# Three held stores behind the last loads in GpSimd's ring, batch 3's first MLP layer in four pieces, the two last stores in halves

## The chip, the cores and the metric

The kernel runs on one core of a Trainium2 chip. The metric is device time in microseconds, the median of several runs. The core has a matmul engine (TensorE, PE), VectorE (DVE), ScalarE (ACT), GpSimd (POOL) and SyncE (SP), and 16 DMA engines that carry what GpSimd's ring (queue q0) and SP's ring (queue q1) hand them.

## The reference

For each of 4 batches, a cross-covariance attention over q, k, v of 6208 x 256, and then a two-layer MLP on the 128 rows with the highest scores:

```python
def _attn_ref(q, k, v, tau):
    qn = q / (np.linalg.norm(q, axis=1, keepdims=True) + 1e-06)
    kn = k / (np.linalg.norm(k, axis=1, keepdims=True) + 1e-06)
    s = kn.transpose(0, 2, 1) @ qn / tau
    ...
    a /= a.sum(-1, keepdims=True) + 1e-09
    return (v @ a).astype(np.float32)

def _moe_ref(x, w_gate, w1, w2, capacity):        # capacity 128
    ...
        top_idx = np.argpartition(-scores[b], capacity)[:capacity]
        xe = x[b, top_idx]
        h = np.maximum(xe @ w1, 0.0)
        ye = h @ w2
        g = 1.0 / (1.0 + np.exp(-scores[b, top_idx]))
        out[b, top_idx] = x[b, top_idx] + g[:, None] * ye
```

## The kernel before

A batch of 6208 rows is cut into six chunks of 1024 rows (1 MB in f32) and one of 64. The order of chunks is `order = [0, 6, 1, 2, 3, 4, 5]`, so `LAST` is chunk 5 and `order[-2]` chunk 4. `L` is batch 3, `E` batch 2. For each batch all q and k chunks are loaded first and summed into the two Gram products in PSUM (`p1_row`); then the softmax; then all v chunks are loaded, transposed (`p2_transpose`), scored (`p2_score`) and multiplied by the attention matrix (`p2_out`), and ScalarE copies the result to a `stage` tile (L482), from which it is stored. Loads are GpSimd's and convert f32 to bf16 on the way, so a load reads 1 MB and writes 512 KB. The last v chunks of batch 3 are loaded in halves.

When a batch's scores are there, `select_stages` finds the 128 rows, gathers them (L603, GpSimd), runs the MLP on them (L641 to L666) and writes the updated rows to the output with a scatter (L697, GpSimd). The scatter of a batch must wait until the stores of this batch have landed. For batch 3, SP waits for the last transfers (`nop`, L691) before the scatter. The first layer of the MLP has eight matmuls into each of two PSUM tiles of 512 columns; for batch 3 ScalarE evicts the first (L651) and VectorE the second (L653).

Stores are SP's. Those of batches 2 and 3 are held back: none is issued until a certain load has landed (`GATE` in `out_store`, in the kernel before the first half of chunk 4 of batch 3's v). Two chunks of batch 1 (`late`) get their MLP update within the matmuls (`change`, `one_hot`, L479) and are stored last of all, so batch 3's scatter doesn't wait for them. From the gate on, SP's ring gets in order: batch 2's chunk 0 in halves, its 64 rows, its chunks 1 to 5, batch 3's chunk 0, 64 rows, chunk 1, chunks 2 and 3 in quarters, chunks 4 and 5, and the two late chunks of batch 1: fourteen times 1 MB and two small pieces. A ring has eight semaphores in turn, so an issue also waits until the transfer eight issues before it in its ring has landed.

The order of instructions on each engine is made by a planner in the program itself (the loop from L843 on): it keeps clocks of the engines (`vt_clock`) and of the rings (`Rings`) and takes what is due next. `r` in that loop is when the planner expects a piece of input. So a changed constant can move instructions.

Of the kernel before, what the change touches and what calls it, by code (L numbers as in the profile page):

```python
# [14 lines left out]
AF = mybir.ActivationFunctionType  # L15
# [3 lines left out]
P = 128  # L19
# [8 lines left out]
def kernel(  # L28
# [12 lines left out]
    nc = tc.nc  # L41
# [8 lines left out]
    NFC = F // P  # L50
    NFULL = N // CHUNK
    REM = N - NFULL * CHUNK
# [34 lines left out]
    def view(t, b, ci):  # L87
        if t is out:
            rows = outs_of[b][b * N:(b + 1) * N]
            if ci < NFULL:  # L90
                return rows[ci * CHUNK:(ci + 1) * CHUNK].rearrange("(p s) c -> p s c", s=RPP)
            return rows[NFULL * CHUNK:N]
        if ci < NFULL:
            return t[b, ci * CHUNK:(ci + 1) * CHUNK, :].rearrange("(p s) c -> p s c", s=RPP)
        return t[b, NFULL * CHUNK:N, :]


    order = [0, NFULL] + list(range(1, NFULL))
    FIRST, LAST = order[0], order[-1]
    L = B - 1  # L100
    E = B - 2
# [7 lines left out]
    UNIT = 2.46  # L109
# [39 lines left out]
    rings = Rings()  # L149
    vt_clock = {"pe": 0.8, "dve": 0.8, "act": 0.8, "pool": 0.8, "sp": 0.8}  # L150

    def now():
        return vt_clock["pe"]
# [6 lines left out]
    late = [(1, order[-2]), (1, LAST)]  # L160
# [42 lines left out]
    def pump():  # L203
        rings.run(now())
        flying[:] = [key for key in flying if rings.done.get(key, 1.0e9) > now()]
        while nxt_unit[0] < len(units):
            u = units[nxt_unit[0]]
            if in_use[bucket(u)] >= limit[bucket(u)] or len(flying) >= AHEAD:
# [13 lines left out]
                      in_=moe_w1.rearrange("(dc p) f -> p dc f", p=P))  # L222
# [59 lines left out]
    stored = {b: [] for b in range(B)}  # L282
# [4 lines left out]
    gate_done = []  # L287
# [158 lines left out]
    def out_psum():  # L446
        turn[0] += 1
        if acc_dead[0]:
            if turn[0] % 4 == 1:
                return ps_s.tile([P, 2, C], F32, name="s_ps")  # L450
            if turn[0] % 4 == 3:
                return ps_g.tile([P, 4, P], F32, name="g_ps").rearrange("p a c -> p (a c)").rearrange(
                    "p (a c) -> p a c", a=2)
        return ps_o.tile([P, 2, C], F32, name="o_ps")
# [26 lines left out]
                                     stop=pj == m - 1 and cc == 1)  # L481
        nc.scalar.copy(st[:parts, s0 + pair * 2:s0 + pair * 2 + m, :], o_ps[:parts, :m, :])  # L482

    def emit_store(b, ci, parts):
        st = stage_of.pop((b, ci))
        ins = []
        keep = dmas if (b, ci) not in late else []
        if ci < NFULL:
            for h in range(parts):
                rows = slice(h * RPP // parts, (h + 1) * RPP // parts)  # L490
                ins.append(nc.sync.dma_start(out=view(out, b, ci)[:, rows, :], in_=st[:, rows, :]))
        else:
            ins.append(nc.sync.dma_start(out=view(out, b, ci), in_=st[:REM, 0, :]))
        if (b, ci) not in late:
            held[b] -= 1
        keep.extend(ins)
        return ins[0]

    def select_stages(b):
# [32 lines left out]
        for i in range(NSTEP):  # L532
# [16 lines left out]
            for h in range(7):  # L549
# [4 lines left out]
                                    in_=mps[:, 0:7 * NTHR].rearrange("p (s j) -> p j s", s=7),  # L554
# [40 lines left out]
        if b == late[0][0]:  # L595
# [7 lines left out]
        ins = nc.gpsimd.indirect_dma_start(out=vg, out_offset=None, in_=v_flat,  # L603
                                     in_offset=bass.IndirectOffsetOnAxis(ap=idx[:, 0:1], axis=0))
# [23 lines left out]
        for cc in range(2):  # L628
            nc.tensor.matmul(mps[:, 0:C], lhsT=vgt[:, cc, :], rhs=a_sb[:, cc, :], start=cc == 0,
                             stop=cc == 1)  # L630
# [7 lines left out]
        nc.vector.tensor_tensor_reduce(out=scj, in0=xe, in1=wg_bcast, scale=1.0, scalar=0.0,  # L638
                                       op0=ALU.mult, op1=ALU.add, accum_out=ssc)
        h_sb = moe.tile([P, NFC, P], BF16, name="h_sb")  # L640
        for hf in range(NFC // 4):  # L641
            h_ps = out_psum().rearrange("p a c -> p (a c)")
            for f4 in range(4):
                fc = hf * 4 + f4
                for dc in range(2):
                    nc.tensor.matmul(h_ps[:, f4 * P:(f4 + 1) * P], lhsT=w1_sb[:, dc, fc * P:(fc + 1) * P],
                                     rhs=xet[:, dc, :], start=f4 == 0 and dc == 0,
                                     stop=f4 == 3 and dc == 1)
            hv = h_sb[:, hf * 4:(hf + 1) * 4, :].rearrange("p f t -> p (f t)")
            if hf == 0 or b < L:  # L650
                nc.scalar.activation(hv, h_ps, AF.Relu)  # L651
            else:
                nc.vector.tensor_scalar_max(hv, h_ps, 0.0)  # L653
        vt_clock["act"] = max(vt_clock["act"], now() + 0.6) + (0.8 if b == L else 1.4)
        gate = moe.tile([P, 1], F32, name="gate")
        nc.scalar.activation(gate, ssc, AF.Exp, scale=-1.0)
# [2 lines left out]
        for fc in range(NFC):  # L659
            nc.tensor.matmul(y_ps[:, 0, :], lhsT=h_sb[:, fc, :], rhs=w2_sb[:, fc, :], start=fc == 0,  # L660
                             stop=fc == NFC - 1)
# [27 lines left out]
        if b == L:  # L689

            nop = nc.sync.nop()  # L691
            for d in dmas[-20:]:
# [4 lines left out]
        ins = nc.gpsimd.indirect_dma_start(out=outs_of[b][0:(b + 1) * N, :],  # L697
                                           out_offset=bass.IndirectOffsetOnAxis(ap=idx[:, 0:1], axis=0),
                                           in_=upd, in_offset=None)
# [93 lines left out]
    def stage_ready():  # L793
        if len(stage_keys) < ST_BUFS:
            return 0.0
        key = stage_keys[-ST_BUFS]
        if key in stage_free:
            return stage_free[key]
        return rings.landing(("st",) + key) + 0.3

    GATE1 = ("v", E, LAST, 0)
    GATE = ("v", L, order[-2], 0)

    def out_store(b, ci):
        vt_clock["sp"] = max(vt_clock["sp"], vt_clock["act"]) + 0.1
        gate = None
        if (b, ci) == hold1[0]:
            gate = GATE1
        elif b >= E and not gate_done:
            gate_done.append(1)  # L810
            gate = GATE
        if gate:
            vt_clock["sp"] = max(vt_clock["sp"], rings.landing(arrival_key[gate]))
        parts = 1 if ci == NFULL else 4 if b == L and ci in order[3:5] else 2 if 0 < len(gate_done) < 3 else 1
        if gate_done:
            gate_done.append(1)
        key = ("st", b, ci)
        for h in range(parts):
            rings.add(1, vt_clock["sp"] + 0.85, UNIT / parts if ci < NFULL else 0.2, key)
        if (b, ci) not in late:  # L820
            stored[b].append(key)
        st = emit_store(b, ci, parts)
        if gate:
            tc.add_manual_dep(
                st.ins, half_inst[gate].ins.name,
                mybir.DependencyInfo(mybir.DependencyClass.Sync, mybir.DependencyReason.DATA),
                reason="stores behind loads")
# [15 lines left out]
    while True:  # L843
# [11 lines left out]
        if nxt_unit[0] == len(units) and not drained and E in gathered:  # L855
            nc.gpsimd.drain(fusable=False)
            drained = True
        while deferred and (GATE1 if deferred[0] in hold1 else GATE) in half_inst:
            out_store(*deferred.pop(0))
        t = now()  # L860
# [3 lines left out]
        if eat_at < len(eat):  # L864
            kind, u, x = eat[eat_at]
            if u in loaded:
                row = x if kind == "p1" else x[1]
                r = rings.landing(arrival_key[u + (int(row >= RPP // 2),)]) + 0.1
                if acc_dead[0]:
                    r += -0.7 if u == ("v", L, LAST) else 0.7  # L870
                if kind == "p1":
                    if u[2] == FIRST and x == 0:
                        r = max(r, acc_free[0])
                else:
                    r = max(r, min(vt_bank)) if vt_live < VT_BUFS or acc_dead[0] else FAR
                able.append((r, 0.5 if acc_dead[0] else 2, kind))
        if score_at < len(scores):
            b, g = scores[score_at]
            if b in aw_ready and (b, g) in vts:
                able.append((max(aw_ready[b], vt_ready[(b, g)]), 1, "S"))  # L880
        if out_at < len(outs):
            b, g, pr = outs[out_at]
            if b in a_ready and (b, g) in vts and score_at > gs.index(g) + b * len(gs) and (
                    (b, g[0]) not in late or hot):
                r = max(a_ready[b], vt_ready[(b, g)], min(o_bank))
                if g[0] < NFULL and g[1] == 0 and pr == 0:
                    r = max(r, stage_ready())
                if eat_at < len(eat) and eat[eat_at][0] == "p1" and b == E and r < t + 1.0:
                    arr = able[-1][0] if able and able[-1][1] == 2 else FAR
                    if max(r, t) < arr < max(r, t) + 0.5:  # L890
                        r = FAR
# [10 lines left out]
        if fit:  # L902
            r, prio, what = min(fit, key=lambda a: (a[1], a[0]))
# [5 lines left out]
        else:  # L909
            r, prio, what = min(able, key=lambda a: (a[0], a[1]))  # L910
# [8 lines left out]
            t = r  # L919
# [10 lines left out]
        elif what == "p1":  # L930
            _, u, s = eat[eat_at]
# [12 lines left out]
        elif what == "T":  # L944
            _, u, g = eat[eat_at]
# [24 lines left out]
        elif what == "S":  # L970
            b, g = scores[score_at]
# [9 lines left out]
        else:  # L981
            b, g, pr = outs[out_at]
# [50 lines left out]
```

## Time and profile before

| | us |
|---|---|
| median of 3 runs | 258.89 |
| the runs | 258.16, 258.89, 259.0 |
| profiled execution, whole | 257.59 |
| its span, first to last instruction | 255.9 |
| PE busy | 214.0 (84%) |
| ACT busy | 106.5 (42%) |
| DVE busy | 92.4 (36%) |
| POOL busy | 56.9 (22%) |
| GpSimd's ring, share of 16 DMA engines' span | 76.4% |
| SP's ring, the same | 26.7% |
| HBM read and written | 78.91 MB and 25.95 MB, 410 GB/s |

The span is one profiled execution; the runs are timed without a profile. Shares of DMA engines can be a little over 1, because the packets of one engine overlap at their ends. The granted clock of TensorE was 0.977 of full speed over the span.

### The profile page before, as it was taken

The page shows a single profiled execution, that of the slowest core. Times are in us where ns is not written, and L with a number is a line of the kernel's source. Part 1 is how long each engine was busy: PE and PEld are TensorE (multiplying, and loading weights), DVE is VectorE, ACT ScalarE, POOL GpSimd, SP SyncE. Part 2 cuts the span into 40 slices and gives each one's busy share as a digit, 9 for nine tenths or more (in the row PEclk, how much of TensorE's full clock was granted, in tenths as well). Part 3 has the DMA queues.
Part 4 walks back from the last instruction along what each step waited for, and adds up shares of the span by engine and source line. Part 5 has one row for each costly group of instructions (what it writes and reads, how often), then busy time and mean ns, then how long its engine had stood idle before and what let it go on. Part 6 is the DMA issues. An engine that isn't in the chain of part 4 may idle for free.

```text
span 255.9 us, 6666 instructions
## 1 busy us (share of the span) xinstructions
PE 214.0 (84%) x2878; PEld 187.4 (73%) x2878; DVE 92.4 (36%) x409; ACT 106.5 (42%) x186; POOL 56.9 (22%) x106
## 2 busy tenths in 40 slices
PE   0099877899999539989999789899999999999960
PEld 0069767798878539878888678788898878888840
DVE  2000001725552002545645006546751064488130
ACT  3800002754554102584234005774313069697740
POOL 7323110522005100722201404112313310000301
PEclk9999999999999958999999999999999999999996
DMA  6999999999999999999999999999999999999996
GB/s 240 258 216 215 214 214 211 215 207 247 272 318 316 315 295 213 224 215 211 264 279 254 214 210 214 213 272 308 219 213 219 214 209 239 415 423 406 376 425 252
DMA packets 17903, 66.88 MB, mean 261 GB/s; under 512 B 2129, under 2 KB 3666, under 8 KB 15058
## 3 DMA queue, kind: packets, MB, share of 16 engines
q0 software_dynamic: 12672, 38.93, 76.4%
q1 hardware_dynamic: 5202, 27.53, 26.7%
q8 instruction: 22, 0.36, 0.5%
q14 instruction: 7, 0.06, 0.1%
HBM read 78.91 MB, written 25.95 MB: 410 GB/s over the span
## 4 chain that ended last, share of the span: by engine, by line
DMA 60%; PE 26%; issue 4%; DVE 4%; POOL 2%; ACT 1%; POOLq 1%; DVEq 0%
DMA k_ch<-in_k_dram 40%; DMA q_ch<-in_q_dram 17%; PE s_ps L303 4%; PE o_ps L474 4%; PE vt_ps L403 4%; DMA out_dram<-stage 3%; PE g_ps L307 2%; PE g_ps L305 2%; PE sc_ps L440 2%; PE g_ps L474 2%; PE s_ps L474 1%; PE o_ps L841 1%; POOL q_ch L187 1%; PE m_ps L550 1%; ACT e L357 1%
## 5 line engine op out<-in xcount | busy, mean ns | idle before, releaser
L303 PE MATMUL s_ps<-q_ch,k_ch 128*128 128x256 bf16 x384 | 90.6, 280 | 27.8 <-DMA k_ch<-in_k_dram 27.8
L305 PE MATMUL g_ps<-q_ch 128*128 128x128 bf16 x384 | 85.8, 224 | 0.0
L307 PE MATMUL g_ps<-k_ch 128*128 128x128 bf16 x384 | 85.8, 223 | 0.0
L482 ACT COPY stage<-o_ps 128x512 f32<-128x512 f32 x77 | 43.9, 589 | 44.0 <-PE o_ps L474 41.7
L303 PEld LDWEIGHTS <-k_ch 128*128 128x128 bf16 x384 | 38.4, 100 | 30.6 <-DMA k_ch<-in_k_dram 29.8
L307 PEld LDWEIGHTS <-k_ch 128*128 128x128 bf16 x384 | 38.6, 100 | 5.4
L305 PEld LDWEIGHTS <-q_ch 128*128 128x128 bf16 x384 | 38.4, 100 | 0.1
L474 PE MATMUL o_ps<-a_sb,vt_sb 128*128 128x256 bf16 (+1 forms) x250 | 35.5, 272 | 1.0 <-ACT stage L482 0.5
L317 DVE CUSTOM_DVE_ANT_0 junk<-g_ps,ident_f 128x128 f32<-128x128 f32 x16 | 4.7, 291 | 67.4 <-PE g_ps L307 67.0
L474 PEld LDWEIGHTS <-vt_sb 128*128 128x128 bf16 (+1 forms) x264 | 23.7, 97 | 6.6 <-issue 3.3
L403 PE MATMUL vt_ps<-ident_b,v_ch 128*128 128x128 bf16 x360 | 25.4, 219 | 2.8 <-ACT vt_sb L417 2.5
L403 PEld LDWEIGHTS <-v_ch 128*128 128x128 bf16 x384 | 23.2, 97 | 5.1 <-issue 3.9
L313 ACT COPY s_sb<-s_ps 128x512 f32<-128x512 f32 x4 | 2.3, 586 | 56.5 <-PE s_ps L303 56.5
L187 POOL DMA_DIRECT2D v_ch<-in_v_dram x26 | 14.2, 547 | 45.2 <-PE vt_ps L403 18.2
L417 ACT COPY vt_sb<-vt_ps 128x1024 bf16<-128x1024 bf16 (+1 forms) x26 | 22.6, 927 | 2.9 <-PE vt_ps L403 2.9
L187 POOL DMA_DIRECT2D q_ch<-in_q_dram x25 | 13.9, 557 | 29.6 <-DMA q_ch<-in_q_dram 10.0
L841 PE MATMUL o_ps<-w_sb,ident_b 128*128 128x256 bf16 x124 | 18.8, 272 | 0.2 <-ACT h_sb L651 0.2
L187 POOL DMA_DIRECT2D k_ch<-in_k_dram x25 | 13.6, 543 | 23.6 <-DMA v_ch<-in_v_dram 9.6
L603 POOL DMA_INDIRECT vg<-in_v_dram,idx x4 | 4.0, 1008 | 63.2 <-DVE idx L599 33.8
L534 DVE SCALAR_TENSOR_TENSOR cmp<-sc,wl,tab 128x392 bf16<-128x392 f32 x28 | 17.5, 626 | 1.0
L841 PEld LDWEIGHTS <-ident_b 128*128 128x128 bf16 x124 | 10.7, 97 | 1.3 <-issue 0.4
L553 DVE TENSOR_REDUCE cnt<-m_ps 128x8 f32<-128x56 f32 x28 | 6.1, 216 | 15.3 <-PE m_ps L550 14.9
(189 smaller groups left out, 270.7 us busy)
## 6 DMA issues: line engine op xcount, KB each, us to landing
out_dram<-stage SPq DMA_DIRECT2D x21, 1024.0 KB, 10.6
q_ch<-in_q_dram POOLq DMA_DIRECT2D x23, 512.0 KB, 17.2
k_ch<-in_k_dram POOLq DMA_DIRECT2D x23, 512.0 KB, 18.8
v_ch<-in_v_dram POOLq DMA_DIRECT2D x22, 512.0 KB, 14.8
stage<-in_moe_w_dram SPq DMA_DIRECT2D x2, 1024.0 KB, 7.0
out_dram<-stage SPq DMA_DIRECT2D x8, 256.0 KB, 8.1
v_ch<-in_v_dram POOLq DMA_DIRECT2D x4, 256.0 KB, 11.2
out_dram<-stage SPq DMA_DIRECT2D x2, 512.0 KB, 5.3
```

What stands on the lines that cost most here:

```text
L187: ins = nc.gpsimd.dma_start(out=t[:, rows, :], in_=view(src, b, ci)[:, rows, :])
L303: nc.tensor.matmul(s_ps[:, cc, :], lhsT=ks[:, sl], rhs=qs, start=begin and cc == 0, stop=end and cc == 1)
L305: nc.tensor.matmul(g_ps[:, cc, :], lhsT=qs[:, sl], rhs=qs[:, sl], start=begin and cc == 0, stop=False)
L307: nc.tensor.matmul(g_ps[:, 2 + cc, :], lhsT=ks[:, sl], rhs=ks[:, sl], start=False, stop=end and cc == 1)
L403: nc.tensor.transpose(vt_ps[:, cc, j, :parts], in_=vt[:parts, s0 + j, cc * P:(cc + 1) * P], identity=ident_b[:parts, :parts])
L417: nc.scalar.copy(vt_sb[:, :, :n, :parts], vt_ps[:, :, :n, :parts])
L440: nc.tensor.matmul(sc_ps[:parts, first + j, :], lhsT=vt_sb[:, cc, j, :parts], rhs=aw_sb[:, cc, :], start=begin and cc == 0 and j == 0, sto ...
L474: nc.tensor.matmul(o_ps[:parts, pj, :], lhsT=vt_sb[:, cc, j, :parts], rhs=a_sb[:, cc, :], start=pj == 0 and cc == 0, stop=pj == m - 1 and ...
L482: nc.scalar.copy(st[:parts, s0 + pair * 2:s0 + pair * 2 + m, :], o_ps[:parts, :m, :])
L534: nc.vector.scalar_tensor_tensor(out=cmp, in0=sc[:, 0:NCOL, None].to_broadcast([P, NCOL, NTHR]), scalar=wl[:, i, NTHR:NTHR + 1], in1=tab[: ...
L553: nc.vector.tensor_reduce(out=cnt9[:, 0:NTHR], in_=mps[:, 0:7 * NTHR].rearrange("p (s j) -> p j s", s=7), axis=AX.X, op=ALU.add)
L841: nc.tensor.matmul(o_ps[:, 0, :], lhsT=ident_b, rhs=w2_sb[:, 0, :], start=True, stop=True)
```

## The change

There are three edits and one constant.

- `emit_store` takes the queue that issues. The first three stores of batch 2 (chunk 0, now whole, the 64 rows, and chunk 1) are issued by GpSimd, so that they stand in its ring behind the last loads, without a gate. SP's first held store is now batch 2's chunk 2, and its gate is the last half of the last load (`("v", L, LAST, 1)`).
- The first MLP layer of batch 3 (`b == L`) is written in four pieces of 256 columns, each in a PSUM tile of its own; ScalarE evicts pieces 0 and 2, VectorE 1 and 3. The other batches keep two of 512.
- The two late stores of batch 1, the last in SP's ring, go in halves.
- In the planner the expected arrival of the last v chunk is 0.4 us after the estimate instead of 0.7 us before it.

```diff
-    def emit_store(b, ci, parts):
+    def emit_store(b, ci, parts, queue):
...
-                ins.append(nc.sync.dma_start(out=view(out, b, ci)[:, rows, :], in_=st[:, rows, :]))
+                ins.append(queue.dma_start(out=view(out, b, ci)[:, rows, :], in_=st[:, rows, :]))
...
-        for hf in range(NFC // 4):
+        piece = 2 if b == L else 4
+        for hf in range(NFC // piece):
             h_ps = out_psum().rearrange("p a c -> p (a c)")
-            for f4 in range(4):
-                fc = hf * 4 + f4
+            for f4 in range(piece):
+                fc = hf * piece + f4
...
-            hv = h_sb[:, hf * 4:(hf + 1) * 4, :].rearrange("p f t -> p (f t)")
-            if hf == 0 or b < L:
-                nc.scalar.activation(hv, h_ps, AF.Relu)
+            hv = h_sb[:, hf * piece:(hf + 1) * piece, :].rearrange("p f t -> p (f t)")
+            if hf % 2 == 0 or b < L:
+                nc.scalar.activation(hv, h_ps[:, 0:piece * P], AF.Relu)
             else:
-                nc.vector.tensor_scalar_max(hv, h_ps, 0.0)
+                nc.vector.tensor_scalar_max(hv, h_ps[:, 0:piece * P], 0.0)
...
-    GATE = ("v", L, order[-2], 0)
+    GATE = ("v", L, LAST, 1)
+
+    BEHIND = 3
+    behind = []
 
     def out_store(b, ci):
+        if b >= E and len(behind) < BEHIND:
+            behind.append((b, ci))
+            key = ("st", b, ci)
+            vt_clock["pool"] = max(vt_clock["pool"], vt_clock["act"]) + 0.6
+            rings.add(0, vt_clock["pool"] + 1.0, UNIT if ci < NFULL else 0.2, key)
+            stored[b].append(key)
+            emit_store(b, ci, 1, nc.gpsimd)
+            return
...
-        parts = 1 if ci == NFULL else 4 if b == L and ci in order[3:5] else 2 if 0 < len(gate_done) < 3 else 1
-        if gate_done:
-            gate_done.append(1)
+        parts = 1 if ci == NFULL else 4 if b == L and ci in order[3:5] else 2 if (b, ci) in late else 1
...
                 if acc_dead[0]:
-                    r += -0.7 if u == ("v", L, LAST) else 0.7
+                    r += 0.4 if u == ("v", L, LAST) else 0.7
```

On GpSimd, at the end of the loads (`v_ch` are the last v chunks, `vg` is batch 3's gather), the difference of the two programs is:

```order
 L187 DMA v_ch<-in_v_dram 128x2048 x3
 L187 DMA v_ch<-in_v_dram 128x1024 x4
+L491 DMA out_dram<-stage 128x2048
+L493 DMA out_dram<-stage_rem 64x256
+L491 DMA out_dram<-stage 128x2048
 L603 DMA vg<-in_v_dram,idx 128x256
```

Three stores now stand between the last load and the gather of batch 3.

On SP, from batch 1's stores to the end (128x2048 is a whole store of 1 MB, 128x1024 a half, 128x512 a quarter):

```order
 L491 DMA out_dram<-stage 128x2048 x6
 L493 DMA out_dram<-stage_rem 64x256
-L491 DMA out_dram<-stage 128x2048 x3
-L491 DMA out_dram<-stage 128x1024 x2
-L493 DMA out_dram<-stage_rem 64x256
-L491 DMA out_dram<-stage 128x2048 x6
+L491 DMA out_dram<-stage 128x2048 x8
 L493 DMA out_dram<-stage_rem 64x256
 L491 DMA out_dram<-stage 128x2048
 L491 DMA out_dram<-stage 128x512 x8
```

Two halves, a 64-row piece and one whole store have left SP's row; behind what is shown, four whole stores have become two whole ones and four halves.

On VectorE, in batch 3's MLP (`scj` is the gate's dot product, `h_sb` the first layer's output):

```order
 L638 ISA scj,ssc<-xe,wg_bcast 128x256
 L638 ISA ssc 128x1
-L653 TENSOR_SCALAR h_sb<-g_ps 128x512
-L662 TENSOR_SCALAR gate<-gate 128x1
-L663 RECIPROCAL gate<-gate 128x1
-L665 SCALAR_TENSOR_TENSOR upd<-o_ps,gate,xe 128x256
-L1028 UNCONDITIONAL_BRANCH
+L654 TENSOR_SCALAR h_sb<-g_ps 128x256
+L654 TENSOR_SCALAR h_sb<-s_ps 128x256
```

One eviction of 512 columns has become two of 256, and what follows them is the same but for its line numbers.

## Rows read from the trace of the kernel before

**Rows 1.** The page, part 2: busy tenths of the DMA engines in 40 slices.

```profile
DMA  6999999999999999999999999999999999999996
```

**Rows 2.** Stretches: window, us, busy us (x instructions) of PE, PEld, DVE, ACT, POOL, clock, DMA share, GB/s.

```profile
205.00:212.00 7.00, 6.53 (x79) 5.51 (x77) 5.10 (x27) 5.24 (x11) 1.06 (x2) 1.00 1.06 210
214.50:215.00 0.50, 0.50 (x10) 0.48 (x8) 0.00 (x0) 0.50 (x2) 0.00 (x0) 1.00 0.82 152
215.00:215.50 0.50, 0.50 (x12) 0.50 (x10) 0.15 (x1) 0.50 (x3) 0.00 (x0) 1.00 0.75 164
218.50:220.50 2.00, 2.00 (x36) 1.86 (x34) 0.00 (x0) 1.77 (x4) 0.00 (x0) 1.00 1.03 423
220.50:224.00 3.50, 3.40 (x48) 2.38 (x46) 2.38 (x12) 2.37 (x5) 0.00 (x0) 1.00 1.00 412
224.00:230.00 6.00, 6.00 (x78) 5.02 (x78) 4.94 (x19) 5.71 (x13) 0.00 (x0) 1.00 1.02 425
230.00:236.00 6.00, 5.72 (x77) 4.80 (x78) 4.84 (x23) 4.93 (x11) 0.00 (x0) 1.00 1.02 411
238.00:240.50 2.50, 2.50 (x26) 2.23 (x24) 0.00 (x0) 1.64 (x4) 2.02 (x2) 1.00 1.04 391
252.00:254.00 2.00, 0.00 (x0) 0.00 (x0) 0.00 (x0) 0.00 (x0) 0.00 (x0) 0.50 0.64 266
```

**Rows 3.** By tile: two of the last load halves and the first held store half.

```profile
L187 POOL DMA_DIRECT2D v_ch<-in_v_dram x1: 527/527/527, 203.3 to 203.3; - x1
...
DMA to landing us min/median/max: 12.4/12.4/12.4
...
L187 POOL DMA_DIRECT2D v_ch<-in_v_dram x1: 535/535/535, 208.3 to 208.3; - x1
...
DMA to landing us min/median/max: 9.9/9.9/9.9
...
L491 SPq DMA_DIRECT2D out_dram<-stage x1: 332/332/332, 214.6 to 214.6; - x1
DMA to landing us min/median/max: 4.9/4.9/4.9
```

**Rows 4.** The chain that ended last: start us, us, what.

```profile
240.66 8.53 DMA out_dram<-stage
...
250.12 1.20 POOLq L1028
```

**Rows 5.** By tile: the last store, and the landing of batch 3's scatter.

```profile
L491 SPq DMA_DIRECT2D out_dram<-stage x1: 332/332/332, 245.2 to 245.2; - x1
DMA to landing us min/median/max: 8.9/8.9/8.9
...
DMA to landing us min/median/max: 4.1/4.1/4.1
```

**Rows 6.** SP's waits from 205 on: waited for, us in total, times, longest.

```profile
SPq L491 <- DMA v_ch<-in_v_dram: 46.7, 1, 46.7
```

**Rows 7.** Timeline of GpSimd: start us, us, instruction, [idle before <- what ended it].

```profile
207.75 1.06 POOL L187 DMA_DIRECT2D v_ch<-in_v_dram  x2 [3.92 <-PE s_ps L403]
238.17 1.01 POOL L603 DMA_INDIRECT vg<-in_v_dram,idx  x1 [29.36 <-DMA out_dram<-stage]
250.34 0.97 POOL L697 DMA_INDIRECT out_dram<-upd,idx  x1 [9.85 <-DMA out_dram<-stage]
```

**Rows 8.** Timeline of DVE and ACT in batch 3's MLP.

```profile
245.47 0.42 DVE L632 CAST xet<-vt_ps 128x256 bf16<-128x256 f32 x1 [0.47 <-PE vt_ps L622]
245.69 0.37 ACT L634 COPY xe<-m_ps 128x256 f32<-128x256 f32 x1 [0.51 <-PE m_ps L629]
246.67 0.60 ACT L651 ACTIVATE h_sb<-o_ps 128x512 bf16<-128x512 f32 x1 [0.61 <-PE o_ps L646]
247.06 0.69 DVE L653 TENSOR_SCALAR h_sb<-g_ps 128x512 bf16<-128x512 f32 x1 [0.53 <-PE g_ps L646]
248.45 0.48 DVE L665 SCALAR_TENSOR_TENSOR upd<-o_ps,gate,xe 128x256 f32<-128x256 f32 x1 [0.45 <-PE o_ps L660]
```

More of the change, by code (lines that the diff above doesn't have):

```diff
@@ L490, in emit_store @@
                 rows = slice(h * RPP // parts, (h + 1) * RPP // parts)
-                ins.append(nc.sync.dma_start(out=view(out, b, ci)[:, rows, :], in_=st[:, rows, :]))
+                ins.append(queue.dma_start(out=view(out, b, ci)[:, rows, :], in_=st[:, rows, :]))
         else:
-            ins.append(nc.sync.dma_start(out=view(out, b, ci), in_=st[:REM, 0, :]))
+            ins.append(queue.dma_start(out=view(out, b, ci), in_=st[:REM, 0, :]))
         if (b, ci) not in late:
@@ L647, in select_stages @@
                                      rhs=xet[:, dc, :], start=f4 == 0 and dc == 0,
-                                     stop=f4 == 3 and dc == 1)
-            hv = h_sb[:, hf * 4:(hf + 1) * 4, :].rearrange("p f t -> p (f t)")
-            if hf == 0 or b < L:
-                nc.scalar.activation(hv, h_ps, AF.Relu)
+                                     stop=f4 == piece - 1 and dc == 1)
+            hv = h_sb[:, hf * piece:(hf + 1) * piece, :].rearrange("p f t -> p (f t)")
+            if hf % 2 == 0 or b < L:
+                nc.scalar.activation(hv, h_ps[:, 0:piece * P], AF.Relu)
             else:
-                nc.vector.tensor_scalar_max(hv, h_ps, 0.0)
+                nc.vector.tensor_scalar_max(hv, h_ps[:, 0:piece * P], 0.0)
         vt_clock["act"] = max(vt_clock["act"], now() + 0.6) + (0.8 if b == L else 1.4)
@@ L821, in out_store @@
             stored[b].append(key)
-        st = emit_store(b, ci, parts)
+        st = emit_store(b, ci, parts, nc.sync)
         if gate:
```

## The prediction

> **What bounds the kernel now.** I read the page's line of DMA digits first [rows 1]: the 16 DMA engines are busy in all 40 slices but the first and the last. Then the table of stretches for the tail [rows 2]. From 205 to 212 us only loads run (share 1.06, 210 GB/s of what lands in SBUF; a load writes half of the bytes that it reads, 0.524 MB, so one takes 0.524 / 210 = 2.50 us). From 224 to 230 only stores run (1.02, 425 GB/s; one store of 1.049 MB takes 2.47 us). In between there is a gap: the share falls to 0.82 and 0.75 for half a microsecond each, from 214.5 to 215.5. The reader should see that the tail is a drain: the loads end at 218, then fourteen 1 MB stores' worth of bytes goes out at the stores' full rate until 254, and no compute engine is asked for more than the drain can carry.
>
> Next, which landing ends it. The landing of a transfer is that of the last of its 16 shares. The last load half is issued at 208.3 and lands 9.9 us later, at 218.2; the half two before it landed at 203.3 + 12.4 = 215.7; the first held store half lands at 214.6 + 4.9 = 219.5 [rows 3]. The chain of waits ends in stores up to 249.19 us (the last store that batch 3's scatter must wait for), then 0.9 us of GpSimd's waits, then the scatter, issued at 250.34 [rows 4, 7]. The scatter lands at 250.3 + 4.1 = 254.4, the very last store at 245.2 + 8.9 = 254.1 [rows 5]; 1.4 us later the span ends. So the end is the drain's end, with the scatter 0.3 us behind it.
>
> **The change part by part.** The sum is made on the profiled execution (span 255.9 us, 257.59 us in all). The median of the runs shown, 258.89 us, is 1.30 us above it, and I carry the difference in time over to the median.
>
> *Stores behind loads in GpSimd's ring.* Removed from SP: four issues (two halves, the 64-row piece, a whole store). Added to GpSimd: three issues after its last load, which is issued by 208.81; they wait for stages long written and for earlier loads. At about 0.53 us each they stand in the ring by about 211, 7 us before the ring's loads end. Behind them on GpSimd is the gather of batch 3, at 238.17, 27 us later, so the 1.6 us of issuing has cover [rows 7]. What it can give is the gap: (1.06 - 0.82) x 0.5 + (1.06 - 0.75) x 0.5 = 0.28 us of all 16 engines [rows 2]. But that is a mean over engines, and the end is the last engine's. For it: two load halves land in 218.2 - 215.7 = 2.5 us, exactly the 2.50 us of a load with no store about, and the first store half follows in 1.3 us where half of 2.47 would be 1.24 [rows 2, 3]. The last engine had no gap; the idle ones were those that had finished their loads early. So I take 0, and keep -0.28 as the bound.
>
> *SP's gate moves to the last load half.* SP's first held store waited 46.7 us until a load landed [rows 6] and was issued at 214.6 [rows 3]; now it waits for the landing at 218.2, 3.6 us later, and behind this wait stand all of SP's other stores. Cover: the ring's 2.1 MB, 4.95 us of work from the moment an engine ends its loads. The early engines run dry of loads from 214.5 on [rows 2], so they have work until 219.5 or later. On this trace the share was down until 215.5, so SP's first bytes moved at most 0.9 us after the issue. 218.2 plus 0.9 is 219.1: covered, by 0.4 us on the early engines and by 4 us on the last one. Cost 0; without cover it would be about the same 0.28 gap again.
>
> *GpSimd's ring carrying stores.* The trace before has no plain store in that ring. Lower bound 0: a load asks 1 MB of its source in 2.50 us, a store of SP's 2.47, so the engines move a megabyte alike through both. Upper bound: if the ring's rate is 210 GB/s of bytes written, 2.1 MB takes 10.0 us instead of 4.9, +5.1. I take 0, since the nearest row is the one that counts bytes read.
>
> *Halves.* One store less in halves at the start, two more at the end. The stretch with the two halves ran at 423 GB/s, whole stores at 425: 0.01 us a store. In the stretch that holds mostly quarters it was 391, +0.21 us a store [rows 2]. So +0.01, at most +0.2.
> The Trainium skill ("DMA: Bandwidth & Descriptors", section "Anatomy of one DMA") prices each DMA at about 2.0 us fixed plus its bytes, which speaks against more and smaller ones; the trace does not agree for queued ones, as the 1.3 us between the landings of the last load half and of a store half shows. By that rule, laid end to end, one more DMA in all would come to an estimated 2.0 us more.
>
> *Tail.* With smaller pieces in SP's ring the scatter's rows may pass between them. The scatter is 128 rows of 1 KB, 0.13 MB, 0.3 us at 425 GB/s: just what it lands behind the last store. Those bytes must pass anyway, so if it overtakes, the store is later by as much. From 252 to 254 the engines are only 0.64 busy, however [rows 2], so some of the 0.3 us is latency and not work. Range -0.3 to 0; I take half, -0.15.
>
> *MLP in four pieces.* Now: ACT takes 0.60 us for 512 columns from 246.67, DVE 0.69 from 247.06, and the update ends at 248.45 + 0.48 = 248.93. At 256 columns the nearest rows are 0.42 on DVE and 0.37 on ACT [rows 8]. The last eviction still starts near 247.06 but ends at 247.48 instead of 247.75, and the second layer has less behind it: 0.3 to 0.5 us sooner. The scatter then waits as before for the store at 249.19 [rows 4], 0.26 us after the update. Gain now 0; it buys slack if the drain gets shorter. What is late next is the drain, as before.
>
> *Planner's arrival constant.* One ACT eviction of about a microsecond goes to DVE, and one group of score matmuls moves ahead of a transpose, at 217 to 218 us. The stores that this could delay stand in a queue whose landing is some 10 us behind the issue (8.9 at the end [rows 5]). Cost 0.
>
> Sum: 0 + 0 + 0 + 0.01 - 0.15 + 0 + 0 = about -0.15 us. 258.89 - 0.15 = **258.7 us**.
>
> **Rivals.**
> *Everything is recovered.* The gap counts in full (-0.28), the scatter's 0.3 too, and a deeper queue takes out the small dips of the drain: 220.5 to 224 at 412 GB/s and 230 to 236 at 411 instead of 425 are 0.12 + 0.20 = 0.32 us [rows 2]. Sum -0.9: 258.0. Against it: the last engine's landings show no gap. For it: the four pieces keep the update ahead of the store only if the drain does end earlier.
> *GpSimd's ring is slower for stores.* On the other side: +5.1 us, 264.0, if the ring goes by bytes written. It decides at the ring's first store: if two 1 MB stores take over 7 us there, beside SP's. For it: its rate in bytes landed is half of SP's [rows 2]; against it: that half is the conversion to bf16. A partial case, stores cut to smaller pieces at the quarters' price on 2.1 MB, is +0.4: 259.1 and still no change.
> *The selection is late.* If the moved score group puts batch 3's gather back by over 0.26 us plus the MLP's gain, about 0.7 us, the update and not the store holds the scatter. A slip of 1.5 us would be +0.8: 259.7. Against it: GpSimd and DVE have cover there.
> *A fixed price per DMA.* One more DMA laid end to end: 260.9 by the skill's figure above; the rows speak against it.
>
> **How the numbers follow.** A run of this kernel can be told from no change at about 0.3%, 0.78 us. Forecast (no change, 258.2 to 259.2): 0.66. Everything recovered, or more than I see: 0.20, counted as faster. Slower: ring 0.05, late selection 0.05, fixed price 0.01, other 0.03: 0.14. The runs before spread over 0.84 us by themselves (258.16 to 259.0), which the range must take in. 258.0 stands inside it; it leaves out the ring's +5 and the far ends: 257.7 to 259.6.
>
> **What would show it right or wrong.** Right: the share no longer dips at 214.5 to 215.5, the last load half still lands near 218.2, and yet the store that the scatter waits for lands at 249.0 to 249.3 and the last DMA at 254.0 to 254.4. The update ends near 248.5 and still waits for the store. The ring's two stores show packets at 425 GB/s beside SP's. Wrong, on the fast side: the drain ends by 253.5, so the gap was on the last engine after all. Wrong, on the slow side: shares of 1 at well below 425 GB/s from 218 to 223, or a scatter that waits for the update.

## The result: 262.38 us, slower by 1.5%

| | before | after |
|---|---|---|
| median, us | 258.47 | 262.38 |
| lowest to highest of 5 runs | 257.71 to 259.0 | 262.18 to 262.98 |
| span of the profiled execution | 255.9 | 260.3 |

The ratio is 1.0148, with a 95% interval of 1.0116 to 1.018: 3.9 us slower. The prediction was 258.7 us, within 257.7 and 259.6.

The page's DMA line of after shows where. It answers [rows 1]: between the first slice and the last there is now one at 6, where all were at 9.

```profile
DMA  6999999999999999999999999999999996999995
```

The table of stretches of after, with the columns of [rows 2]. The first eight rows answer rows there; the last three cut the hole up further.

```profile
214.50:215.00 0.50, 0.50 (x6) 0.39 (x5) 0.00 (x0) 0.50 (x2) 0.00 (x0) 1.00 1.16 213
215.00:215.50 0.50, 0.50 (x10) 0.49 (x9) 0.00 (x0) 0.50 (x2) 0.00 (x0) 1.00 1.17 221
218.50:220.50 2.00, 2.00 (x37) 1.86 (x35) 0.81 (x2) 0.89 (x2) 0.00 (x0) 1.00 0.54 217
220.50:224.00 3.50, 3.40 (x52) 2.57 (x48) 2.20 (x10) 2.38 (x6) 0.90 (x2) 1.00 1.00 410
224.00:230.00 6.00, 6.00 (x76) 4.93 (x75) 4.96 (x21) 5.70 (x12) 0.77 (x2) 1.00 1.00 406
230.00:236.00 6.00, 5.03 (x74) 4.27 (x72) 4.78 (x23) 3.51 (x9) 0.00 (x0) 1.00 1.01 386
238.00:240.50 2.50, 2.50 (x27) 2.25 (x25) 0.64 (x4) 2.04 (x5) 1.00 (x1) 1.00 0.99 410
252.00:254.00 2.00, 0.35 (x2) 0.00 (x0) 0.48 (x1) 0.00 (x0) 0.00 (x0) 0.91 1.02 418
...
216.00:217.00 1.00, 0.69 (x16) 0.57 (x14) 0.98 (x2) 1.00 (x3) 0.00 (x0) 1.00 0.64 119
217.00:218.00 1.00, 1.00 (x36) 1.00 (x34) 0.76 (x2) 0.73 (x2) 0.00 (x0) 1.00 0.30 55
218.00:219.00 1.00, 1.00 (x36) 1.00 (x34) 0.85 (x2) 0.00 (x0) 0.00 (x0) 1.00 0.12 23
```

The old dip at 214.5 to 215.5 is gone from its place. A far deeper one stands from 216 to 219.5: the share is 0.64, 0.30, 0.12. The loads run out and no store is there to follow. Behind the hole a stretch moves between 6% less and 5% more than the same one before, and the run of stores ends some 4 us later.

Why no store was there is in the timeline of GpSimd of after (columns as in [rows 7]), which answers [rows 7]:

```profile
208.09 1.06 POOL L187 DMA_DIRECT2D v_ch<-in_v_dram  x2 [3.97 <-PE s_ps L403]
223.10 0.54 POOL L491 DMA_DIRECT2D out_dram<-stage  x1 [13.96 <-ACT stage L482]
223.64 0.55 POOL L493 DMA_DIRECT2D out_dram<-stage_rem  x1
224.19 0.58 POOL L491 DMA_DIRECT2D out_dram<-stage  x1
239.22 1.00 POOL L603 DMA_INDIRECT vg<-in_v_dram,idx  x1 [14.44 <-DMA out_dram<-stage]
```

The three stores are issued at 223.1 to 224.8, 14 us behind the last load. The timeline names ScalarE's copy as the releaser, but that tile had long been written: with the drain moved (below), the last of the three is issued at 211.39. What stands between is an instruction that the timeline doesn't list, since it runs on GpSimd's sequencer (`POOLq`): a drain of GpSimd's ring, `nc.gpsimd.drain(fusable=False)` (L856 of before, L867 of after). The planner emits it in the same round of its loop as the stores, and ahead of them. By line (count: duration in ns min/median/max, first and last start), after and then before:

```profile
L867 POOLq DRAIN  x1: 13990/13990/13990, 208.5 to 208.5; - x1
```

```profile
L856 POOLq DRAIN  x1: 13891/13891/13891, 208.2 to 208.2; - x1
```

In the kernel before it filled part of the 29.4 us in which GpSimd seemed idle ahead of the gather [rows 7], so it cost nothing. It ends 3.8 us after the last load has landed, in both kernels (222.0 behind 218.2, 222.5 behind 218.6). In the changed kernel the stores queue behind it until 222.5.

The chain's end (answers [rows 4]) has the same two pieces, 4 us later:

```profile
244.61 8.80 DMA out_dram<-stage
...
254.01 1.20 POOLq L1039
```

### The profile page after: what moved, and what is told of

Same layout as the page of the kernel before. It is cut to its first block, busy times and chain, and to the rows that moved or that the text cites. A ratio compares the mean times of both kernels' runs of the same rounds, so it can differ in the third digit from the quotient of the medians.

```text
span 260.3 us, 6670 instructions
## 1 busy us (share of the span) xinstructions
PE 216.4 (83%) x2878; PEld 189.4 (73%) x2878; DVE 93.4 (36%) x411; ACT 105.4 (40%) x186; POOL 58.5 (22%) x109
## 4 chain that ended last, share of the span: by engine, by line
DMA 65%; PE 20%; issue 5%; POOL 4%; DVE 3%; ACT 1%; POOLq 1%; DVEq 0%; ACTq 0%
DMA k_ch<-in_k_dram 48%; DMA q_ch<-in_q_dram 9%; DMA out_dram<-stage 8%; PE s_ps L303 5%; PE g_ps L307 3%; PE g_ps L305 3%; PE o_ps L474 2%; PE vt_ps L403 2%; POOL q_ch L187 1%; PE s_ps L474 1%; PE sc_ps L440 1%; PE g_ps L474 1%; POOL k_ch L187 1%; PE o_ps L479 1%; POOL v_ch L187 1%
## 5 line engine op out<-in xcount | busy, mean ns | idle before, releaser
L187 POOL DMA_DIRECT2D v_ch<-in_v_dram x26 | 14.1, 544 | 44.8 <-PE vt_ps L403 17.5
L187 POOL DMA_DIRECT2D q_ch<-in_q_dram x25 | 13.9, 554 | 29.9 <-DMA q_ch<-in_q_dram 9.1
L534 DVE SCALAR_TENSOR_TENSOR cmp<-sc,wl,tab 128x392 bf16<-128x392 f32 x28 | 17.5, 627 | 1.0
## 6 DMA issues: line engine op xcount, KB each, us to landing
out_dram<-stage POOLq DMA_DIRECT2D x2, 1024.0 KB, 13.9
out_dram<-stage SPq DMA_DIRECT2D x8, 256.0 KB, 13.6
```

Source lines behind the costliest of these rows:

```text
L187: ins = nc.gpsimd.dma_start(out=t[:, rows, :], in_=view(src, b, ci)[:, rows, :])
L534: nc.vector.scalar_tensor_tensor(out=cmp, in0=sc[:, 0:NCOL, None].to_broadcast([P, NCOL, NTHR]), scalar=wl[:, i, NTHR:NTHR + 1], in1=tab[: ...
```

## The experiments

Two things differ in after ahead of the hole: SP's gate is later, and the stores that were to cover this are held up by the drain. The theory under test: the drain's place is the cause, the late gate the price. The rivals: the gate alone, stores being slow in GpSimd's ring, or stage buffers that come back late. Each ratio below is to the kernel before.

**The drain behind the three stores.** The changed kernel with

```diff
-        if nxt_unit[0] == len(units) and not drained and E in gathered:
+        if nxt_unit[0] == len(units) and not drained and E in gathered and len(behind) == BEHIND:
```

> The changed kernel with one edit: GpSimd's drain, which stands behind the last load and ahead of the three stores that it issues, is put behind those stores; nothing else moves on any engine. The profile of the changed kernel has the drain at 208.5 for 13.99 us and the stores behind it at 223.1 to 224.2. Theory A (the drain holds the stores back, so the rings run empty at 215.5 to 219.6 and a stage buffer comes back late at 235.2): the three stores are issued by about 211, land by about 225, the DMA share stays over 0.75 at 215 to 219.5, ScalarE no longer waits 2.3 us for a store at 235, and the time falls by 3.4 to 4.2 us against the changed kernel, to 258.2 to 259.0, a ratio of 0.998 to 1.003 to the kernel before. Rival B (the later gate on SP's first store is the cost, the drain only a bystander): SP's store still goes out at 218.7, some 2.8 us of mean share stay lost, and the time stays at 260.5 or more. Rival C (stores in GpSimd's ring are slow or are served late whenever they are issued): they land after 230 though issued by 211, ScalarE still waits at 235, and the time stays near 262.

258.82 us, ratio 1.0019 (0.9992 to 1.0046): of the 3.9 us, 0.5 are left, and the interval reaches below none. GpSimd's timeline, two stretches, and what the DMA engines carried from 218 to 220:

```profile
207.87 1.05 POOL L187 DMA_DIRECT2D v_ch<-in_v_dram  x2 [3.92 <-PE s_ps L403]
208.90 0.54 POOL L491 DMA_DIRECT2D out_dram<-stage  x1
209.44 0.55 POOL L493 DMA_DIRECT2D out_dram<-stage_rem  x1
211.39 0.58 POOL L491 DMA_DIRECT2D out_dram<-stage  x1 [1.40 <-ACT e L357]
```

```profile
216.00:218.00 2.00, 1.78 (x50) 1.78 (x50) 1.74 (x4) 1.51 (x4) 0.00 (x0) 1.00 1.09 350
218.00:220.00 2.00, 2.00 (x38) 1.87 (x36) 1.09 (x2) 0.61 (x2) 0.00 (x0) 1.00 1.01 422
...
DMA packets 130, 0.84 MB, mean 422 GB/s; under 512 B 21, under 2 KB 21, under 8 KB 32
q0 software_dynamic: 130, 0.84, 101.4%
```

The stores are issued by 212, and the rings stay full. From 218 to 220 all packets are those of GpSimd's ring (q0), and they move at 422 GB/s, as fast as SP's stores (425 before). SP's gate is as late as in after and costs nothing now. So neither the gate by itself nor the ring by itself is the cause.

**The gate alone.** The kernel before with

```diff
-    GATE = ("v", L, order[-2], 0)
+    GATE = ("v", L, LAST, 1)
```

> The kernel before with the gate alone: SP's first held store waits for the second half of the last load, not for the first half of the one before; no store goes into GpSimd's ring, the MLP and the last stores stay as they were. Theory A: with no store in GpSimd's ring the gate leaves the same empty stretch as in the changed kernel (the engine that ends last is idle from 218.2 to 219.2, the mean engine loses some 2.8 us against 0.28 us before), so the time rises by 1.0 to 2.8 us, to 259.5 to 261.3; the rest of the changed kernel's 3.9 us is then the late stores' holding of stage buffers. Rival B (the gate alone is the whole cost): 262 to 262.8. Rival E (the held stores have slack, so a later gate costs nothing and all comes from the three stores): 258.2 to 258.8.

262.04 us, 1.0128 (1.0087 to 1.017), +3.9 us. The whole loss of the changed kernel is there without any store in GpSimd's ring. That is rival B's figure, and above the 1.0 to 2.8 us that I expected: what an uncovered gate costs was still priced too low. Together with the run above: the late gate is the price, and the drain is why it had to be paid.

**The gate part of the way.** The same edit with `("v", L, LAST, 0)`:

> The kernel before with SP's gate moved by half as much: to the first half of the last load, not its second half (which cost 3.9 us) and not the first half of the one before. Theory A (each engine that has done its loads stands idle until the gate lets SP's store go, and the lost bytes are never made up since the rings stay full to the end): the gate opens about 1.23 us later than before, and a part of the 3.9 us shows: 1.0 to 2.5 us, ratio 1.004 to 1.010. Rival K (there is a threshold: the cost comes from one event at the late gate, as a stage buffer that comes back too late): the ratio is under 1.002 or over 1.013.

260.97 us, 1.0114 (1.0075 to 1.0153), +2.9 us: three quarters of the cost. It is not half of the way, though. The gate of the kernel before is the first half of chunk 4, issued at 201.6. The half that landed at 215.7 [rows 3] is the second one of that chunk, and the expectation took it for the gate. By tile, in the kernel before, the gate of before and then this run's:

```profile
L187 POOL DMA_DIRECT2D v_ch<-in_v_dram x1: 528/528/528, 201.6 to 201.6; - x1
...
DMA to landing us min/median/max: 12.9/12.9/12.9
...
L187 POOL DMA_DIRECT2D v_ch<-in_v_dram x1: 530/530/530, 207.7 to 207.7; - x1
...
DMA to landing us min/median/max: 9.2/9.2/9.2
```

So the gates are at 214.5, 216.9 and 218.2. This run's opens 2.4 us later than before, not 1.23, and that is two thirds of the whole way of 3.7 us. The ratio is above theory A's 1.004 to 1.010, which was made for 1.23 us, though its interval reaches into that. Rival K's figures (under 1.002, over 1.013) miss the ratio too, though its interval reaches past 1.013; three quarters of the cost at two thirds of the way speak for a cost that grows with the way, and not for a threshold.

The bytes account for most of the cost. For four kernels, the mean GB/s (last column) in 214 to 222 and in 222 to 252. Before:

```profile
214.00:222.00 8.00, 7.69 (x148) 6.95 (x146) 3.83 (x10) 6.43 (x12) 0.00 (x0) 1.00 1.02 349
222.00:252.00 30.00, 25.05 (x279) 20.38 (x276) 14.95 (x64) 19.82 (x41) 2.99 (x3) 0.99 1.02 409
```

After:

```profile
214.00:222.00 8.00, 7.69 (x148) 7.00 (x146) 4.31 (x9) 5.52 (x11) 0.00 (x0) 1.00 0.71 202
222.00:252.00 30.00, 26.60 (x282) 21.90 (x278) 14.84 (x65) 19.96 (x42) 3.69 (x5) 0.95 1.02 397
```

The gate alone:

```profile
214.00:222.00 8.00, 7.63 (x152) 7.12 (x153) 3.77 (x9) 6.39 (x11) 0.00 (x0) 1.00 0.65 165
222.00:252.00 30.00, 26.18 (x288) 21.28 (x285) 15.00 (x64) 20.62 (x43) 2.02 (x2) 1.00 1.02 402
```

The gate part of the way:

```profile
214.00:222.00 8.00, 7.61 (x145) 6.89 (x143) 4.40 (x12) 5.98 (x12) 0.00 (x0) 1.00 0.81 255
222.00:252.00 30.00, 25.25 (x280) 20.66 (x280) 14.38 (x60) 20.07 (x42) 2.02 (x2) 0.99 1.02 405
```

Up to 222, after has moved (349 - 202) x 8 = 1180 kB less than before; at 420 GB/s that is 2.8 us. From 222 to 252 it is (409 - 397) x 30 = 360 kB, 0.9 us. Sum 3.7 of the 3.9 measured. The gate alone: 3.5 + 0.5 = 4.0, measured 3.9. Part of the way: 1.8 + 0.3 = 2.1, measured 2.9; these are means over the engines, and the 0.8 us between stays open. Of the first terms, 0.4 us of the gate alone and 0.2 us of after are there because the last loads of these executions landed later (219.1 and 218.6, against 218.2 in the other two), and loads move 210 GB/s where stores move 420. Since the share is 1.02 over the whole of 222 to 252 in all of them, there is no room to make up a byte that isn't moved before 222.

**The gate of before, stores still behind the drain.** The changed kernel with

```diff
+    LANDED = ("v", L, order[-2], 0)
...
-            gate = GATE
+            gate = LANDED
```

> The changed kernel with one edit: SP's first held store waits for the half load that the kernel before waited for (which landed at 215.7 there), not for the last one. The drain still holds the three stores in GpSimd's ring until 223. It separates the two things that go wrong in the changed kernel: the empty stretch, which the late gate opens (the gate alone in the kernel before gave 262.0, a ratio of 1.013), and the three stores' lateness. Theory A (the empty stretch is nearly all of it): SP's queue fills the stretch as before, the rings are full from 214.6, and the time is 258.3 to 259.2, ratio 1.000 to 1.004. Rival C (the late stores hold stage buffers, ScalarE waits for one at 235): that wait stays, and the time is 260 or more.

259.09 us, 1.0054 (1.0027 to 1.0081). (The half load that this gate waits for landed at 214.5 in the kernel before, not at 215.7.) The hole is closed by SP (348 GB/s from 214 to 222), and ScalarE's wait for a stage buffer is gone, which theory C said would stay. The median is within theory A's times, the ratio a little above its 1.004. The run doesn't separate the two things cleanly: the planner made another order of PE's work with it, the gather comes 2 us later than in the kernel before, and TensorE's granted clock is 0.68 and then 0.50 (1.2 GHz) in the two stretches from 248 to 252, in which the MLP runs, behind 2 us with only 0.57 us of matmuls. Now the update holds the scatter, 2.8 us behind the store at 249.84:

```profile
252.19 0.48 DVE L666 SCALAR_TENSOR_TENSOR upd<-o_ps,gate,xe 128x256 f32<-128x256 f32 x1 [1.02 <-PE o_ps L661]
252.96 0.97 POOL L698 DMA_INDIRECT out_dram<-upd,idx  x1 [10.48 <-DMA out_dram<-stage]
```

That the three late stores cost something of their own is not shown. In after, ScalarE did wait for one (columns of the timeline), but since after loses no more than the gate alone does, within the intervals, this wait stood beside full rings:

```profile
235.31 0.58 ACT L482 COPY stage<-s_ps 128x512 f32<-128x512 f32 x1 [2.30 <-DMA out_dram<-stage]
```

**No drain.** The changed kernel, and the kernel before, without this line:

```diff
-            nc.gpsimd.drain(fusable=False)
```

> The changed kernel without GpSimd's drain. Theory A (the drain's place is the cost): as with the drain behind the stores, 258.2 to 259.0. If the drain itself also holds back the gather for batch 2 or anything later, it is lower than that kernel by over 0.3 us; by the profile of the kernel before, where the drain ends at 222.0 and GpSimd then stands idle until 238.2, it is not. Rival B (the later gate): 260.5 or more. Rival C (stores in GpSimd's ring are slow): near 262.

> The kernel before without GpSimd's drain, so that its price there is measured by itself. Theory A: nothing on GpSimd stands between the drain's end at 222.0 and the gather at 238.2, so the time is that of the kernel before within 0.3 us (ratio 0.999 to 1.001). Rival D (the drain does something for the transfers behind it: without it the gather has to bring its ring up to date itself): the gather at 238.2 takes longer than 1.0 us or lands later, and the time rises by 1 us or more.

263.74 us, 1.021 (1.0165 to 1.0255), and 263.07 us, 1.0169 (1.0128 to 1.021). No theory had this cause. (The gather at 238, which the expectation calls batch 2's, is batch 3's.) By their figures, rival B fits the first (260.5 or more) and rival D the second (1 us or more, and a gather that lands later: 8.1 us behind its issue, 5.7 in the kernel before). But in the changed kernel the hole was closed all the same (373 GB/s from 214 to 222), so B's reason is out; and its gather landed 6.1 us behind its issue, while the gate alone, with its drain in place, has one of 7.9. Most of the loss stands behind everything: from the landing of the last scatter to the end of the span it is 5.4 and 6.8 us, and 1.4 in the kernel before. The kernel before without its drain has a last scatter that lands at 253.1 + 2.8 = 255.9, and a span of 262.8. Its last scatter (first the row of both scatters, then their landing times) and its closing drains, by line, and then the closing drains of the kernel before:

```profile
L697 POOL DMA_INDIRECT out_dram<-upd,idx x2: 975/994/1013, 240.6 to 253.1; - x2
...
DMA to landing us min/median/max: 2.8/5.4/7.9
```

```profile
L1025 POOLq DRAIN  x3: 51/97/9127, 252.8 to 262.5; - x3
...
L1028 POOLq DRAIN  x3: 51/97/4485, 250.1 to 255.6; - x3
```

The program ends with a drain of GpSimd anyway (the longest of the three). In the kernel before this one takes 4.49 us and ends 0.2 us after the last landing. Without the early drain it takes 9.13 us and ends 6.0 us after it. So the early drain does work that must be done once, at a time when GpSimd has nothing else to do.

**The drain later.** The drain stands behind batch 2's scatter instead, on the kernel with the stores in GpSimd's ring and MLP and last stores as before:

```diff
+        if nxt_unit[0] == len(units) and not drained and E in scattered and L in gathered:
...
+        scattered.add(b)
```

> The kernel with the three stores in GpSimd's ring, the late gate and the MLP and last stores of before, but with GpSimd's drain moved from behind the three stores to behind batch 2's scatter, where GpSimd otherwise waits some 10 us for the last stores. Without any drain there the one at the kernel's end took 9.1 and 9.4 us, against 4.5 us with one, and the time rose by 4.9 us. Theory I (the drain is work that GpSimd does once for all transfers since the last drain, some 9 us when all but the newest have landed): it runs from about 240.6 to about 250, just before the last scatter at 251.2, the one at the end stays at 4.5 to 5 us, and the time is that of the same kernel with the drain earlier, a ratio to the kernel before of 0.997 to 1.001. Rival J (it takes 14 us or more wherever it stands): it ends at 254.5 or later, the last scatter goes out 3 us late, and the time rises to 261 or more.

257.89 us, 0.9999 (0.9979 to 1.0019). Theory I. The drain starts at 239.0, as the sequencer runs ahead, and ends at 250.6, 0.3 us ahead of the store that the last scatter waits for (250.89):

```profile
L868 POOLq DRAIN  x1: 11539/11539/11539, 239.0 to 239.0; - x1
```

**The small parts, each alone on the kernel before.** The MLP in four pieces (`piece = 2 if b == L else 4`), and the last stores in halves (`2 if (b, ci) in late or ...`):

> The kernel before with batch 3's first MLP layer in four pieces of 256 columns and nothing else. Theory A: the update is ready at 248.9 and is wanted at 250.1 by the last scatter, so whatever the pieces do within 1 us either way is not seen: ratio 0.999 to 1.001. Rival F (the pieces change the planner's order ahead of the MLP enough to delay the last stores): above 1.002.

> The kernel before with the two last stores in halves and nothing else. In the changed kernel the halved stores moved 418 GB/s against 426 for whole ones. Theory A: two stores at 2.46 us become 2.50 each, +0.1 us, ratio 1.000 to 1.001. Rival G (halves let each transfer begin earlier, so the last lands earlier): they only start while the ring is full, so no gain; if it is there, the ratio is under 0.999.

0.9993 (0.9973 to 1.0014) and 1.0009 (0.9993 to 1.0026). Neither can be told from no change.

**The change with its fault mended, in two forms.** Stores in GpSimd's ring and the drain behind them, MLP and last stores as before, timed twice; then with the MLP's pieces and whole stores:

> The kernel before with the three stores in GpSimd's ring behind the last loads, the drain behind them, and the late gate; the MLP and the last stores stay as they were before. It is the version that might beat both: it fills the dip of 0.28 us that the kernel before has at 214.5 to 215.5 and doesn't pay for halves. Theory A: 0 to 0.3 us under the kernel before, 257.9 to 258.3, ratio 0.998 to 1.001. Rival H (the wait of 0.28 us was not on the path that ends last, or the stores delay the last half load by as much): ratio 1.000 or more, and the last half load lands later relative to its issue than the 9.93 us of the kernel before.

> The same kernel as with the ring alone (three stores in GpSimd's ring, the drain behind them, the late gate, MLP and last stores of before), timed once more on its own, since its ratio of 0.998 reached from 0.997 to 1.000. Theory A (it recovers the dip of about 0.3 us that the kernel before has ahead of 216): 0.997 to 1.000 again. Rival H (no gain): 1.000 or more.

> The changed kernel with the drain behind the three stores and the two last stores whole again: all of the change but its halves, which cost a ratio of 1.001 alone. Theory A: as the ring alone, 0.997 to 1.000, since the MLP's pieces have slack. Rival F (the pieces cost): over 1.001.

257.69 us, 0.9984 (0.9967 to 1.0001); again 258.1 us, 0.9999 (0.9979 to 1.0019); 258.05 us, 0.9986 (0.9963 to 1.0009). All three lie at or a little below the kernel before, and none of them beats it beyond the interval.

The whole time has a part outside the span, and the change makes it longer. It is 1.66 to 1.78 us in all executions of the kernel before, 1.91 to 2.01 in the first form and 2.02 to 2.09 in the second; the changed kernel itself has 2.03 to 2.08, the MLP's pieces alone 1.89 to 1.98, the halves alone and the gate alone what before has. The spans of the three runs are shorter: medians of 255.7, 256.1 and 256.0 us, against 256.4. So by these medians the forms gain 0.3 to 0.7 us within the span, in the order of the dip of 0.28 us, and lose some 0.3 us of it again outside. Why that part grows is not shown.

## Why the prediction was wrong, point by point

- **"At about 0.53 us each they stand in the ring by about 211."** This is the step that failed. [rows 7] shows no instruction of GpSimd between 208.8 and 238.17, and I took the time as free. The sequencer was busy with a drain for 13.9 us of it, in the source a few lines from what the change touches and with a row of its own in the trace. With the drain behind the stores they were issued by 212, about as the step said.
- **"Covered, by 0.4 us on the early engines."** The arithmetic of the cover held wherever the stores were in the ring: with the drain moved, the late gate cost nothing measurable.
- **"Without cover it would be about the same 0.28 gap again."** Mis-sized by more than ten times: 3.9 us (the gate alone). The 0.28 is what is left with the gate at a landing at 214.5. With the gate at the last landing, engines that have ended their loads stand idle until the last load is in, and then until SP's store is issued: against 1.06, the shares of after lack 0.42 + 0.76 + 0.94 us in the three microseconds from 216 alone. The range held nothing of this term, though the rows had a better bound: SP's first store moves by 218.2 - 214.6 = 3.6 us, as the prediction says itself [rows 3], in which up to 16 engines could be idle.
- **Ring carrying stores, 0.** Right: 422 GB/s in GpSimd's ring. The rival at 264.0 came near the time measured without being its cause.
- **The gap, 0 with -0.28 as the bound.** Right as far as the times tell: no ratio of the mended forms is clear of 1. By the medians of the spans the bound may be nearer.
- **The difference in time carried over to the median.** The sum was made on the span, and what lies outside it was taken as unchanged. It grew by about 0.35 us, a term that the sum did not have.
- **The dips of the drain, 0.12 + 0.20.** The first is 0.11 by the same rows; nothing hangs on it.
- **Halves, +0.01 to +0.2.** Not contradicted: a ratio of 1.0009 (0.9993 to 1.0026), which can't be told from none. The Trainium skill's price for one DMA of GpSimd's path ("DMA: Bandwidth & Descriptors", section "Anatomy of one DMA") would, if it held for SP's halves, make the two more transfers of that run an estimated 4 us, laid end to end; the run does not agree.
- **Tail, -0.15.** Not there. With halves the scatter still lands 0.3 to 0.5 us behind the last store, as before.
- **MLP, 0.3 to 0.5 us sooner, gain 0.** Right, where the clock is the same. With the clock at full speed in both, from the cast of `xet` to the end of the update takes 2.98 us in the last form above and took 245.47 to 248.93 = 3.46 [rows 8]. In after itself it took 4.5, with TensorE's granted clock at 0.50 (1.2 GHz) from 250 to 252, and still ended 0.55 us ahead of the store at 253.42. The last form above:

```profile
245.66 0.42 DVE L632 CAST xet<-vt_ps 128x256 bf16<-128x256 f32 x1 [0.47 <-PE vt_ps L622]
...
248.16 0.48 DVE L666 SCALAR_TENSOR_TENSOR upd<-o_ps,gate,xe 128x256 f32<-128x256 f32 x1 [0.23 <-PE o_ps L661]
```

- **Planner's constant, 0.** Nothing speaks against it: with the drain moved, the gather is issued at 238.19, against 238.17.
- **The chances.** 0.14 stood on slower, and of what came true, that the stores don't get into the ring in time, no rival spoke. "That the change doesn't do what it says" was the case to price.

## What to carry to other kernels

When work is put onto an engine that looks idle, list every instruction of its sequencer there, drains and waits too: an idle gap of a timeline only says that no data moved. When a cover is what makes a moved wait free, price the wait without the cover and keep that as the bound. With DMA rings that are full to the end, count bytes by stretch: what isn't moved in a hole is the loss.

## What the hardware showed that was not expected

A drain of GpSimd costs time of its own, and this time goes with the number of DMAs that GpSimd has issued since the drain before it. In the twelve runs that have an early drain, both drains end behind the last landing of GpSimd's ring by about 0.041 us for each of these DMAs, and 0.04 us more (DMAs counted in the traces):

| DMAs since the drain before | end behind the last landing, us | which drains |
|---|---|---|
| 1 | 0.08 | closing, where the early one stands late |
| 3 | 0.16 | closing, nine runs |
| 6 | 0.29 | closing, the two runs with three stores behind the early drain |
| 93 | 3.85 | early, seven runs |
| 96 | 3.97 | early, the four runs with three stores ahead of it |
| 98 | 4.05 | early one that stands late |

The rest of a drain's length is the time up to that landing: the early ones took 13.8 to 14.5 us, 17.5 to 17.8 with the stores ahead, and 11.5 when late; the closing ones took 3.0 to 5.0 us. So the early drain pays for some 90 DMAs while GpSimd has nothing else to do. Where there was none, the closing drain had 96 and 99 DMAs behind it, began only 3.1 and 4.7 us ahead of the last landing, took 9.1 and 9.4 us, and ended 6.0 and 4.7 us after that landing. That is 2.1 and 0.6 us more than the sizes above would make it. What a drain does in this time is not shown.
